# Order of the transposes, the value products and the weight sums in a fused attention and MLP kernel

## The chip, the cores and the metric

The kernel runs on one core of a Trainium2 chip. The core has five engines that run side by side, each taking its own instructions strictly in the order in which the program gives them: PE (TensorE, matmuls and transposes through the matrix array), DVE (VectorE), ACT (ScalarE), POOL (GpSimd) and SP (SyncE, which here only issues DMAs). An instruction waits until what it needs is ready, and everything behind it on its engine waits with it. The metric is device time in microseconds of the whole kernel; lower is better. The time before is 350.78 us, the median of three runs (350.43 to 350.84).

## The reference

```python
# 8 batches, 8 heads, 576 positions, head size 64
scores = scale * np.matmul(q, k.transpose(0, 1, 3, 2))
log_f = np.log(np.clip(f, 0.0001, 1.0))
cum = np.cumsum(log_f, axis=-1)
decay = cum[:, :, :, None] - cum[:, :, None, :]
scores = np.where(causal, -1000000000.0, scores + decay)
attn = np.exp(scores - np.max(scores, axis=-1, keepdims=True))
attn = attn / (np.sum(attn, axis=-1, keepdims=True) + 1e-09)
attn_out = np.matmul(attn, v)
# heads side by side: x is 4608 tokens x 512
h = x @ w_in          # 512 x 2048
g = h - np.tanh(h)
return g @ w_out      # 2048 x 512
```

## The kernel before

Attention goes by pairs of heads: 8 batches of 4 pairs, 32 in all, and each pair has a *slot* p (0 to 31; slot 32 finishes the last pair). The MLP runs in pieces between the attention's instructions, so that PE always has something to do.

**What a slot does.** For its pair it computes the scores in seven tiles, called s0 to s6 here (`scores`, L332 on PE): one or two matmuls into a PSUM bank, then an exp on ACT (L348). From slot 5 on, POOL sets the exp's upper triangle to zero (L359); in slots 0 to 4 a second matmul does the masking (L340). For the pair of the slot before, `values` multiplies the exps with v: two halves, va and vb, 15 matmuls each (L369), into one PSUM tile `av` of which there is a single buffer. Behind vb stand three DVE instructions (L375 to L377), here called the values chain: sums, their reciprocal, and `xn`, the normalised output. `turn` brings xn to the other orientation into `XR`: in batch 0 by five PE transposes and a DVE copy (L387, L388), later by two DMA transposes on SP's queue (L390, L392).

**Turns of q and k.** The scores need q and k with the head size on partitions. For batches 0 to 2, `trans` does this for the *next* pair: six PE transposes (L284) into a PSUM bank, then two copies, one for each head, into `QT` or `KT`, on DVE (L294, "VV") or ACT (L292, "AA" for slots 7 and 8; the very first two turns are split into four copies). From slot 4 on there is one such bank, `tr`, so a turn waits until the one before it is copied out; x's transposes in slot 4 use it as well. From batch 3 on, DMAs do the turning.

**The MLP.** Its work is a list of steps, 30 for each block of 512 tokens: 16 hidden tiles (`mlp1`: four matmuls L404, tanh on ACT L411, an addition `gt` on DVE L417, behind every fourth tile two more DVE sums L431) and 14 products (`product`, L452, eight matmuls each). The hidden tiles' PSUM banks `mb` are three in rotation; the tanh output has two buffers. The second matrix product is a fast algorithm in seven products for 2x2 blocks, n = 1 to 7, two row groups each. It needs four differences of blocks of w_out, which `wsum` makes once, on DVE (L266), in halves: sum 0 and, from it, sum 2 (for product 6), sum 1 (for product 7) and sum 3 (for product 4). They are put behind steps 16, 17, 19 and 21, both halves of a sum at once. `settle` (L469 to L483) takes the products out of PSUM; the results go through the tile `ost`, which has two buffers, to a DMA on SP's queue.

**The order.** Everything is emitted in an order written out by hand, and each engine takes its own in that order. Slots 0 to 4 follow the lists `FIRST`, whose entries `first_slot` decodes: s and g are score tiles and groups of them, q and k turns (the digit says how many slots ahead the pair is), va and vb the values, x the `turn` of the slot before and y that of two slots before, h0 to h2 the first three matmuls of the first three hidden tiles, m a step of the MLP, p memsets, r and c constant rows, and a number so many matmuls that only keep PE busy ("spins", L271). From slot 5 on, `att_items` lists a slot's entries: score tiles, loads, turns (in slots 5 to 10), va, vb and turn behind the second tile; and 6 steps (7 in slots 9 and 10, then 7 or 8) are spread evenly among those entries that count: the score tiles, the turns, vb and turn. By this rule, in slot 5 steps stand behind s1, turn, q's turn, s4, k's turn and s6. The products of the first block of tokens are steps 16 to 29: step 16 is the last of slot 6, 17 to 22 are slot 7's, 23 to 28 slot 8's, and step 29 is the first of slot 9.

Of the kernel before, what the change touches and what calls it, by code (L numbers as in the profile page):

```python
# [17 lines left out]
FAR = 3  # L18
# [4 lines left out]
def kernel(  # L23
# [18 lines left out]
    NPAIR = H // 2  # L42
# [4 lines left out]
    NFT = DFF // P  # L47
# [24 lines left out]
    K2, E2, T2 = NFT // 2, DM // 2, UW // 2  # L72
# [6 lines left out]
    qn, kn = ([t[0:S // NT6, :].rearrange("p (h n d) -> p h n d", h=H, n=NT6) for t in raw] for raw in (qraw, kraw))  # L79
    qb, kb = ([t[:, 0:NJ * DM].rearrange("p (n e) -> p n e", n=NJ) for t in raw] for raw in (qraw, kraw))  # L80
    vn = [qkp.tile([P, NJ, H, VW], FP16, tag=f"vn{i}", name=f"vn{i}") for i in range(2)]
    QT = [qkp.tile([D + 3, H, S], FP16, tag=f"QT{i}", name=f"QT{i}") for i in range(2)]
    KT = [qkp.tile([D + 3, H, PITCH], FP16, tag=f"KT{i}", name=f"KT{i}") for i in range(2)]
# [195 lines left out]
    def trans(b, c, src, dst, engs):  # L279
        pn, g3 = S // NT6, NT6 // 2  # L280
        t16 = t_bank().bitcast(FP16)[:, 0:2 * S // 2].rearrange("p (a g n) -> p a g n", a=2, g=g3)
        for a in range(2):
            for g in range(g3):
                nc.tensor.transpose(out=t16[:, a, g, :], in_=src[b % 2][:, 2 * c + a, 2 * g:2 * g + 2, :],  # L284
                                    identity=id16[0:pn, 0:pn])
        for a0, an in ((0, 1), (1, 1)) if len(engs) > 2 else ((0, 2),):
            for e in range(2):
                h0 = 2 * c + a0
                to = dst[b % 2][0:D, h0:h0 + an, 0:S].rearrange("d a (g e p) -> d a g e p", g=g3, e=2)[:, :, :, e, :]
                of = t16[e * D:(e + 1) * D, a0:a0 + an, :, :]  # L290
                if engs[2 * a0 + e] == "A":
                    nc.scalar.activation(out=to, in_=of, func=AF.Copy)  # L292
                else:
                    nc.vector.tensor_copy(out=to, in_=of)  # L294
            if a0 == 0 and engs == "AAAA":
                cum_q()
# [65 lines left out]
    def values(b, c, a):  # L362
        if a == 0:
            av = ps_av.tile([P, 2, 512], FP32, tag="av", name="av")
            AV[(b, c)] = av[:, :, 0:NJ * (D + 1)].rearrange("p a (i d) -> p a i d", i=NJ)
        av = AV[(b, c)]
        for ib in range(NJ):
            for j in range(ib + 1):
                nc.tensor.matmul(out=av[:, a, ib, :], lhsT=E.pop((b, c, a, j, ib)),  # L369
                                 rhs=vn[b % 2][:, j, 2 * c + a, 0:D + 1], start=(j == 0), stop=(j == ib))  # L370
        if a == 0:
            return
        xn = XN[(b, c)] = fin.tile([P, NJ, P], FP16, tag="xn", name="xn")
        rs = fin.tile([P, 2, NJ, 1], FP32, tag="rs", name="rs")
        nc.vector.tensor_scalar_add(out=rs, in0=av[:, :, :, D:D + 1], scalar1=1e-9)  # L375
        nc.vector.reciprocal(out=rs, in_=rs)
        nc.vector.tensor_tensor(out=xn.rearrange("p i (a d) -> p a i d", a=2), in0=av[:, :, :, 0:D],  # L377
                                in1=rs.to_broadcast([P, 2, NJ, D]), op=ALU.mult)

    def turn(b, c):  # L380
        xn = XN.pop((b, c))
        r0 = b % 3 * S
        if b == 0:
            xt = t_bank().bitcast(FP16)[:, 0:S]
            for ib in (NJ - 1, 0, 1, 2, 3):
                w0 = min(ib * P, S - P)
                nc.tensor.transpose(out=xt[:, w0:w0 + P], in_=xn[:, ib, :], identity=id16)  # L387
            nc.vector.tensor_copy(out=XR[:, c, r0:r0 + S], in_=xt)  # L388
            return
        nc.sync.dma_start_transpose(out=XR[:, c, r0:r0 + S - D].rearrange("p (n t) -> p n t", t=P),  # L390
                                    in_=xn[:, 0:NJ - 1, :].rearrange("p n d -> p (n d)"))
        nc.sync.dma_start_transpose(out=XR[:, c, r0 + S - D:r0 + S], in_=xn[D:P, NJ - 1, :])  # L392
# [96 lines left out]
    mlp = []  # L489
    for u in range(NU):  # L490
        mlp += [[(mlp1, u, ft)] for ft in turns]
        mlp += [[(product, u, n, g)] for n, g in ((1, 0), (1, 1), (2, 0), (6, 0), (6, 1), (2, 1))]
        mlp += [[(product, u, n, g)] for n in (5, 7, 3, 4) for g in range(2)]
    for at, n in ((NFT, 0), (NFT + 1, 2), (NFT + 3, 1), (NFT + 5, 3)):
        mlp[at] += [(wsum, n, 0, K2 // 2), (wsum, n, K2 // 2, K2)]

    STEPS = [0]

    def step():
        for fn, *args in mlp[STEPS[0]]:  # L500
            fn(*args)
        STEPS[0] += 1

    FIRST = [["8", "q0", "k0", "5", "s0", "s1", "q1", "s2", "k1", "p", "s4", "s5", "q2", "s6", "s3"],
# [4 lines left out]

    def first_slot(p):  # L510
        here = pairs[p]
        before = pairs[p - 1] if p else None
        for what in FIRST[p]:
            kind, arg = what[0], what[1:]
# [29 lines left out]
    def att_items(p):  # L544
        items = []
        before = pairs[p - 1]
        after = pairs[p + 1] if p + 1 < len(pairs) else None
        for ti in range(len(TILES)):
            if p < len(pairs):
                items.append((lambda ti=ti: scores(*pairs[p], (ti,), "late"), True))  # L550
            items += [(load, False) for load in LOADS.get((p, ti), ())]
            if ti in (3 if p == 2 * NPAIR - 1 else 2, 5) and after and after[0] < FAR:
                dst, src = (KT, kn) if ti == 5 else (QT, qn)
                items.append((lambda dst=dst, src=src: trans(*after, src, dst, "AA" if 2 * NPAIR - 1 <= p <= 2 * NPAIR else "VV"), True))
            if ti == 1:
                items += [(lambda a=a: values(*before, a), a == 1) for a in range(2)]
                items.append((lambda: turn(*before), True))
        return items

    with tc.manual_schedule(engines={PE, mybir.EngineType.Pool, mybir.EngineType.SP, mybir.EngineType.DVE,  # L560
                                     mybir.EngineType.Activation}):
        with tc.tile_pool(name="ps_t2", bufs=1, space=PSUM) as POOLS["t"]:
            with tc.tile_pool(name="ps_one", bufs=4, space=PSUM) as POOLS["s"]:
                first_slot(0)
            with tc.tile_pool(name="ps_two", bufs=2, space=PSUM) as POOLS["s"]:
                for p in range(1, NPAIR):
                    first_slot(p)
        del POOLS["t"]
        POOLS["s"] = ctx.enter_context(tc.tile_pool(name="ps_sc", bufs=2, space=PSUM))
        POOLS["m"] = ctx.enter_context(tc.tile_pool(name="ps_m", bufs=3, space=PSUM))  # L570
        first_slot(NPAIR)
        for p in range(NPAIR + 1, len(pairs) + 1):
            items = att_items(p)
            take = 6 if p <= 2 * NPAIR else 7 if p == 2 * NPAIR + 1 or p % 2 == 0 else 8
            whole, given, n = sum(c for _, c in items), 0, 0
            for emit, counts in items:
                emit()
                n += counts
                while given < take and (given + 1) * whole <= n * take and STEPS[0] < len(mlp):
                    step()  # L580
                    given += 1
        while STEPS[0] < len(mlp):
            step()
# [28 lines left out]
```

## Time and profile before

| what | us |
|---|---|
| median of three runs | 350.78 |
| the profiled execution, its own time | 350.38 |
| its span, from the first to the last instruction | 348.7 |
| PE busy | 334.7 (96%) |
| DVE busy | 253.3 (73%) |
| ACT busy | 220.2 (63%) |
| POOL busy | 176.9 (51%) |

The profile page shows one execution. A line of the timeline has the start, the duration, the engine, the line of the kernel, the operation, what is written and read, and the count where instructions in a row are merged; a bracket at its end says how long the engine was idle before it and what released it. Matmuls are pipelined and their ends are modelled, so that neighbouring ones overlap in the records: idle time is best read from the starts. The second part of the page cuts the span into 40 slices of 8.7 us and gives the busy share in tenths:

```profile
PE   7898998998999999999999999999999999999996
DVE  7576889819896589748984889388937863873872
ACT  6564876777765786568756875588558843623631
PEclk9989999999999999999999999999999999999999
```

PE's thinner slices are among the first ten, besides the last; DVE's row has one slice of 1, the ninth.

### The profile page before, as it was taken

The page shows a single profiled execution, that of the slowest core. Times are in us where ns is not written, and L with a number is a line of the kernel's source. Part 1 is how long each engine was busy: PE and PEld are TensorE (multiplying, and loading weights), DVE is VectorE, ACT ScalarE, POOL GpSimd, SP SyncE. Part 2 cuts the span into 40 slices and gives each one's busy share as a digit, 9 for nine tenths or more (in the row PEclk, how much of TensorE's full clock was granted, in tenths as well). Part 3 has the DMA queues.
Part 4 walks back from the last instruction along what each step waited for, and adds up shares of the span by engine and source line. Part 5 has one row for each costly group of instructions (what it writes and reads, how often), then busy time and mean ns, then how long its engine had stood idle before and what let it go on. Part 6 is the DMA issues. An engine that isn't in the chain of part 4 may idle for free.

```text
span 348.7 us, 8658 instructions
## 1 busy us (share of the span) xinstructions
PE 334.7 (96%) x3295; PEld 234.1 (67%) x3295; DVE 253.3 (73%) x523; ACT 220.2 (63%) x412; POOL 176.9 (51%) x322
## 2 busy tenths in 40 slices
PE   7898998998999999999999999999999999999996
PEld 2585556774578656887886568756887786487475
DVE  7576889819896589748984889388937863873872
ACT  6564876777765786568756875588558843623631
POOL 8967179875277726774667457753222220500500
PEclk9989999999999999999999999999999999999999
DMA  9999999999589998999699979994122013003003
GB/s 100 145 181 176 195 180 136 131 168 208 83 65 119 179 149 80 116 168 175 65 120 141 180 87 110 156 168 74 47 83 46 19 34 122 0 12 111 3 0 122
DMA packets 169560, 38.82 MB, mean 111 GB/s; under 512 B 155906, under 2 KB 169454, under 8 KB 169518
## 3 DMA queue, kind: packets, MB, share of 16 engines
q0 software_dynamic: 116576, 18.36, 87.2%
q1 hardware_dynamic: 52942, 19.90, 29.1%
q8 instruction: 26, 0.43, 0.6%
q14 instruction: 16, 0.13, 0.1%
HBM read 36.85 MB, written 9.44 MB: 133 GB/s over the span
## 4 chain that ended last, share of the span: by engine, by line
PE 78%; DVE 12%; DMA 4%; ACT 3%; issue 2%; SPq 1%; POOL 0%; DVEq 0%; ACTq 0%; POOLq 0%
PE mb L404 29%; PE px L452 16%; PE mb L452 12%; PE ps L332 11%; PE av L369 7%; DVE gt L417 4%; DMA out_dram<-ost 2%; DVE KT L294 2%; DVE sm L431 2%; DVE xn L377 1%; DMA kn<-in_k_dram 1%; ACT th L411 1%; ACT e L348 1%; PE t L284 1%; DVE QT L294 1%
## 5 line engine op out<-in xcount | busy, mean ns | idle before, releaser
L404 PE MATMUL mb<-XR,win 128*128 128x512 f16 (+4 forms) x704 | 141.6, 340 | 1.0 <-DVE gt L417 0.7
L348 ACT ACTIVATE e<-ps 128x512 f16<-128x512 f32 (+1 forms) x183 | 109.3, 617 | 28.2 <-PE ps L332 15.7
L411 ACT ACTIVATE th<-mb 128x512 f32<-128x512 f32 x144 | 86.3, 600 | 50.8 <-PE mb L404 46.5
L417 DVE TENSOR_TENSOR gt<-mb,th 128x512 f16<-128x512 f32 x144 | 97.1, 686 | 25.2 <-ACT th L411 24.4
L359 POOL TENSOR_SCALAR_AFFINE_SELECT e<-e 128x128 f16<-128x128 f16 x162 | 59.7, 372 | 104.5 <-ACT e L348 103.9
L404 PEld LDWEIGHTS <-win 128*128 128x128 f16 x704 | 61.8, 97 | 49.2 <-issue 2.8
L332 PE MATMUL ps<-QT,KT 67*128 67x64 f16 (+4 forms) x384 | 75.4, 279 | 4.3 <-DVE KT L294 1.4
L452 PEld LDWEIGHTS <-gt 128*128 128x128 f16 x576 | 53.8, 97 | 10.9 <-DVE gt L417 1.1
L332 PEld LDWEIGHTS <-KT 67*128 67x128 f16 x384 | 36.3, 99 | 26.4 <-DVE KT L294 3.4
L452 PEld LDWEIGHTS <-sm 128*128 128x128 f16 x432 | 40.4, 97 | 7.2 <-DVE ws L266 0.6
L452 PE MATMUL mb<-ws,gt 128*128 128x256 f16 x288 | 36.4, 272 | 0.0
L482 DVE TENSOR_TENSOR ost<-mb,part 128x512 f32<-128x512 f32 x25 | 17.1, 685 | 25.9 <-PE mb L404 6.8
L369 PEld LDWEIGHTS <-e 128*128 128x128 f16 x896 | 32.9, 98 | 3.7 <-DVE xn L377 0.9
L369 PE MATMUL av<-vn,e 128*128 128x65 f16 x896 | 34.4, 194 | 0.7 <-DVE xn L377 0.7
L469 ACT ACTIVATE part<-px 128x512 f32<-128x512 f32 x24 | 14.3, 597 | 30.1 <-PE px L452 30.1
L452 PE MATMUL px<-ws,sm 128*128 128x256 f16 x256 | 31.6, 272 | 0.0
L113 POOL DMA_DIRECT2D vn<-in_v_dram x32 | 28.7, 905 | 2.4 <-issue 1.9
L377 DVE TENSOR_TENSOR xn<-av,rs 128x640 f16<-128x640 f32 x32 | 26.4, 824 | 1.1
L431 POOL TENSOR_TENSOR sm<-gt 128x512 f16<-128x512 f16 x4 | 4.6, 1152 | 36.3 <-DVE gt L417 36.3
L94 POOL DMA_DIRECT2D qn<-in_q_dram x25 | 21.8, 872 | 1.5 <-issue 1.4
L94 POOL DMA_DIRECT2D kn<-in_k_dram x25 | 21.4, 854 | 1.2 <-issue 0.9
L452 PE MATMUL mb<-wout,gt 128*128 128x256 f16 x160 | 21.4, 272 | 0.0
(83 smaller groups left out, 302.6 us busy)
## 6 DMA issues: line engine op xcount, KB each, us to landing
out_dram<-ost SPq DMA_DIRECT2D x34, 256.0 KB
vn<-in_v_dram POOLq DMA_DIRECT2D x32, 128.0 KB, 5.9
qn<-in_q_dram POOLq DMA_DIRECT2D x20, 128.0 KB, 3.8
kn<-in_k_dram POOLq DMA_DIRECT2D x20, 128.0 KB, 4.7
win<-in_moe_w_in_dram POOLq DMA_DIRECT2D x4, 512.0 KB, 8.6
wout<-in_moe_w_out_dram POOLq DMA_DIRECT2D x2, 1024.0 KB, 16.3
qn<-in_q_dram POOLq DMA_DIRECT2D x10, 144.0 KB, 7.4
kn<-in_k_dram POOLq DMA_DIRECT2D x10, 144.0 KB, 7.1
```

The costliest lines, as they stand in the source:

```text
L94: nc.gpsimd.dma_start(out=dst[b % 2][0:pn, n, :].rearrange("p (h d) -> p h d", h=H), in_=src[b, :, n * P:n * P + pn, :].rearrange("h p d - ...
L113: nc.gpsimd.dma_start(out=vn[b % 2][:, n, h0:h1, 0:D], in_=v[b, h0:h1, n * P:(n + 1) * P, :].rearrange("h p d -> p h d"))
L332: nc.tensor.matmul(out=ps[:, col:col + n], lhsT=KT[b % 2][0:D + 3, h, j * P:(j + 1) * P], rhs=QT[b % 2][0:D + 3, h, i0:i0 + n], start=True ...
L348: nc.scalar.activation(out=eb[:, :, lo:hi], in_=banks[:, 0:n2, lo:hi], func=AF.Exp, scale=qscale)
L359: nc.gpsimd.affine_select(out=view, in_=view, compare_op=ALU.is_ge, fill=0.0, base=0, pattern=pat, channel_multiplier=-1)
L369: nc.tensor.matmul(out=av[:, a, ib, :], lhsT=E.pop((b, c, a, j, ib)), rhs=vn[b % 2][:, j, 2 * c + a, 0:D + 1], start=(j == 0), stop=(j == ib))
L377: nc.vector.tensor_tensor(out=xn.rearrange("p i (a d) -> p a i d", a=2), in0=av[:, :, :, 0:D], in1=rs.to_broadcast([P, 2, NJ, D]), op=ALU. ...
L404: nc.tensor.matmul(out=hps[:, o:o + n], lhsT=win[:, ci, ft * P:(ft + 1) * P], rhs=XR[:, ci, t:t + n], start=(ci == 0), stop=(ci == NCH - 1))
L411: nc.scalar.activation(out=th, in_=hps, func=AF.Tanh, scale=-1.0)
L417: nc.vector.tensor_tensor(out=GT[(u, ft)], in0=hps, in1=th, op=ALU.add)
L452: nc.tensor.matmul(out=ps[:, g * E2:(g + 1) * E2], lhsT=left(k), rhs=right[:, k, :], start=(first and (g == 0 or last) and k == 0), stop=( ...
L482: nc.vector.tensor_tensor(out=ost, in0=ps, in1=PART.pop((u, {2: 1, 7: 5, 4: 6}[n])), op=ALU.add)
```

## The change

Five places change, all in the order of emission; every computation stays.

- At the start, 3 spins behind k's first turn instead of 5.
- In slots 2 and 3, vb is emitted ahead of k's turn instead of behind it.
- In slot 4, x comes ahead of h2 and q's turn (it stood behind both), and k's turn ahead of the third step instead of behind it.
- In slots 5 to 10, q's turn comes behind the second score tile, ahead of the values (it stood behind the third tile; in slot 7 behind the fourth), and k's behind the fifth tile (it stood behind the sixth). The steps between them fall in other places by the rule of even spreading: in slots 5 to 8 behind s1, vb, s2, s4, s5 and s6; in slots 9 and 10 behind s1, vb, turn, s3, s4, s5 and s6.
- The halves of each weight sum go to two successive steps: sum 0 to steps 14 and 15 (both were behind 16), sum 2 to 16 and 17 (17), sum 1 to 19 and 20 (19), sum 3 to 22 and 23 (21).

```diff
-    for at, n in ((NFT, 0), (NFT + 1, 2), (NFT + 3, 1), (NFT + 5, 3)):
-        mlp[at] += [(wsum, n, 0, K2 // 2), (wsum, n, K2 // 2, K2)]
+    for at, n in ((NFT - 2, 0), (NFT, 2), (NFT + 3, 1), (NFT + 6, 3)):
+        for o in range(2):
+            mlp[at + o] += [(wsum, n, o * K2 // 2, (o + 1) * K2 // 2)]
...
-    FIRST = [["8", "q0", "k0", "5", "s0", "s1", "q1", "s2", "k1", "p", "s4", "s5", "q2", "s6", "s3"],
+    FIRST = [["8", "q0", "k0", "3", "s0", "s1", "q1", "s2", "k1", "p", "s4", "s5", "q2", "s6", "s3"],
              ["g0", "g1", "k1", "g3", "va", "r", "vb", "q2", "g2"],
-             ["g0", "y", "va", "g1", "k1", "vb", "g3", "q2", "g2"],
-             ["g0", "y", "va", "g1", "k1", "vb", "g3", "g2"],
-             ["c", "va", "s0", "y", "vb", "s1", "h0", "h1", "q1", "h2", "x", "s2", "m", "s3", "m", "s4", "m", "k1", "s5", "m", "s6", "m"]]
+             ["g0", "y", "va", "g1", "vb", "k1", "g3", "q2", "g2"],
+             ["g0", "y", "va", "g1", "vb", "k1", "g3", "g2"],
+             ["c", "va", "s0", "y", "vb", "s1", "h0", "h1", "x", "h2", "q1", "s2", "m", "s3", "m", "s4", "k1", "m", "s5", "m", "s6", "m"]]
...
-            if ti in (3 if p == 2 * NPAIR - 1 else 2, 5) and after and after[0] < FAR:
-                dst, src = (KT, kn) if ti == 5 else (QT, qn)
+            if ti in (1, 4) and after and after[0] < FAR:
+                dst, src = (KT, kn) if ti == 4 else (QT, qn)
                 items.append((lambda dst=dst, src=src: trans(*after, src, dst, "AA" if 2 * NPAIR - 1 <= p <= 2 * NPAIR else "VV"), True))
```

## The prediction

> **What bounds the kernel now.** The page first (its lines on engines and slices, above), then the busy time of the engines by stretch: PE, PEld, DVE, ACT, POOL, then the granted clock, DMA share and GB/s. Then the timelines of PE, DVE and ACT up to 95 us.
>
> ```profile
> 0.00:31.00 31.00, 26.16 (x311) 17.78 (x312) 20.68 (x58) 19.07 (x29) 25.72 (x36) 0.94 1.86 146
> 31.00:95.00 64.00, 59.11 (x590) 37.79 (x589) 49.77 (x102) 45.62 (x88) 39.58 (x71) 1.00 2.02 161
> 95.00:348.00 253.00, 249.41 (x2397) 178.56 (x2396) 182.84 (x365) 155.52 (x296) 111.61 (x216) 1.00 0.87 95
> ```
>
> PE idles 4.8 us before 31 us and 4.9 us in 31 to 95, where all the edits lie; behind 95 us it is busy 98.6% of the time with code that doesn't change. So whatever slot 11 starts earlier or later by is the change of the total. At most about 9 us are to be had.
>
> ```profile
> 37.50:47.65 10.15, 9.49 (x87) 5.10 (x85) 9.81 (x20) 8.43 (x17) 5.50 (x11) 1.00 1.39 201
> 47.65:56.30 8.65, 8.14 (x82) 5.04 (x83) 7.54 (x16) 6.10 (x13) 6.63 (x13) 1.00 2.68 153
> 56.30:68.10 11.80, 10.55 (x127) 8.36 (x126) 11.59 (x23) 8.51 (x17) 10.56 (x17) 1.00 3.07 131
> 68.10:78.60 10.50, 9.90 (x133) 8.04 (x129) 1.90 (x4) 6.94 (x13) 7.98 (x15) 1.00 2.34 157
> ```
>
> The third busy column is DVE. In slots 5 to 7 (37.5 to 68.1 us) it is busy 28.9 of 30.6 us: reordering its queue there gains only what ends its few idle spells. In slot 8 it is nearly idle, and that is a wait, not rest (below).
>
> **The change part by part.** I follow one shift from slot to slot: minus is earlier than before. A turn's two DVE copies take 0.91 us, one values chain on DVE (rs, its reciprocal and xn: from 23.9 to 25.2 below) 1.2 us, half a weight sum 0.68 us.
>
> *Two spins fewer.*
>
> ```profile
> 7.22 2.33 PE L271 MATMUL spin<-ones 128*128 128x512 f16 x5
> 7.46 1.28 DVE L294 COPY KT<-t 64x288 f16<-64x288 f16 x4
> 9.34 0.63 PE L332 MATMUL ps<-QT,KT 67*128 67x512 f16 x1
> 6.88:10.29 3.41, 3.41 (x14) 1.48 (x14) 1.71 (x5) 1.45 (x4) 3.41 (x6) 1.00 2.27 148
> ```
>
> Spins start 0.42 us apart (9.34 less 7.22 over 5), so three end at 8.49; k's copies are done at 8.74, and s0 starts at 8.79 instead of 9.34. But these matmuls run at half rate until 10.29 (the same 67x512 matmul shows 0.63 us here and 0.38 in the row at 24.37 below), so s0's three wide ones just fill the time: s1 starts at 10.2, not 10.52, partly slow. Shift -0.28. PE is unbroken from there to the next copies, so it lasts into slot 2.
>
> *Values ahead of k's turn, slots 2 and 3.*
>
> ```profile
> 22.94 0.92 DVE L294 COPY KT<-t 64x576 f16<-64x576 f16 x2 [0.87 <-PE t L284]
> 24.35 0.82 DVE L377 TENSOR_TENSOR xn<-av,rs 128x640 f16<-128x640 f32 x1
> 24.37 0.38 PE L332 MATMUL ps<-QT,KT 67*128 67x512 f16 x1
> 29.34 0.59 PE L369 MATMUL av<-vn,e 128*128 128x65 f16 x14 [0.70 <-DVE xn L377]
> 29.80 0.38 PE L332 MATMUL ps<-QT,KT 67*128 67x512 f16 x1
> ```
>
> DVE takes k's copies, then the values chain; now the other way round. With vb ended at 22.85 the chain runs from 22.9 to 24.1 and the copies end at 25.0. Slot 3's first scores need them: 25.06 instead of 24.37, +0.69. In slot 3 everything follows; its chain ends at 28.87 instead of 29.29, so slot 4's va no longer waits 0.70 us, but k's copies end at 29.7 and s0 of slot 4 starts at 29.8 as before. What the spin gave is used up: shift 0.
>
> *x ahead of h2 and q1, k1 ahead of a step, slot 4.*
>
> ```profile
> 31.46 0.82 DVE L377 TENSOR_TENSOR xn<-av,rs 128x640 f16<-128x640 f32 x1
> 32.38 0.42 PE L284 MATMUL t<-id,qn 96*128 96x96 f16 x6
> 33.82 0.45 PE L387 MATMUL t<-id,xn 128*128 128x128 f16 x5 [0.37 <-DVE QT L294]
> 34.65 0.60 ACT L348 ACTIVATE e<-ps 128x512 f16<-128x512 f32 x1 [2.77 <-PE ps L340]
> 37.50 0.69 DVE L417 TENSOR_TENSOR gt<-mb,th 128x512 f16<-128x512 f32 x1 [0.29 <-ACT th L411]
> ```
>
> q1 and x share one PSUM bank, and x now waits for q's copies. With x at 32.38 (its xn is ready at 32.28), its copy ends at 33.33, under h2; q1 follows at 33.38 and s2 at 33.64 instead of 34.11. ACT, which is packed from 34.65 on, starts 0.47 earlier. Then k's copies go ahead of the third gt and fill the 0.29 us that DVE waited there. Together -0.47 - 0.29 = -0.76, and DVE stays packed to slot 5's end: K ready for slot 6 at -0.73.
>
> *q behind the second tile, k behind the fifth; weight sums in parts.*
>
> ```profile
> 47.68 0.61 PE L332 MATMUL ps<-QT,KT 67*128 67x512 f16 x3 [0.45 <-DVE KT L294]
> 54.10 0.41 PE L284 MATMUL t<-id,kn 96*128 96x96 f16 x6 [0.48 <-DVE QT L294]
> 57.96 1.38 DVE L266 TENSOR_TENSOR ws<-wout 128x1024 f16<-128x1024 f16 x2
> 59.60 1.37 DVE L266 TENSOR_TENSOR ws<-wout,ws 128x1024 f16<-128x1024 f16 x2
> 59.91 0.60 ACT L348 ACTIVATE e<-ps 128x512 f16<-128x512 f32 x1 [1.46 <-PE ps L332]
> 60.34 1.29 PE L452 MATMUL mb<-ws,sm 128*128 128x256 f16 x8 [0.47 <-DVE ws L266]
> 64.69 1.30 ACT L292 ACTIVATE KT<-t 64x576 f16<-64x576 f16 x2
> 66.05 0.39 PE L332 MATMUL ps<-QT,KT 67*128 67x512 f16 x1 [0.39 <-ACT KT L292]
> 68.88 0.17 DVE L375 TENSOR_SCALAR rs<-av 128x10 f32<-128x10 f32 x1 [0.85 <-PE av L369]
> ```
>
> The waits of k's trans for q's copies (0.48 us in slot 6, shorter in 7, 9 and 10) go. But k's copies keep their place among DVE's instructions (behind four gts, ahead of two), so with DVE packed the next slot's start gains nothing: PE waits for K instead. In slot 6 the first half sum (step 14) even enters ahead of them: +0.68 less rounding, slot 7 starts at -0.13. The work isn't lost. DVE reaches the second half of sum 2 at 60.2 instead of 60.99 (-0.8), and PE, with q already turned, meets no wait at 60.34. In slot 7 both turns are copied on ACT: q now in an idle spell (ACT waited 1.46 us ahead of 59.91), k at 62.5 to 63.8 instead of 64.69 to 66.0, so slot 8's s0 starts about 64.4 (its bank waits for the sixth exp) instead of 66.05, its vb ends about 67.3, q's 0.26 us included. DVE, packed, is free at 67.25. The values chain of slot 8 starts at 67.33 instead of 68.88: **-1.55**.
>
> *What hangs on it.*
>
> ```profile
> 72.79 5.76 DMA out_dram<-ost
> 81.24 0.60 ACT L411 ACTIVATE th<-mb 128x512 f32<-128x512 f32 x1 [0.76 <-DVE gt L417]
> 85.70 0.61 PE L332 MATMUL ps<-QT,KT 67*128 67x512 f16 x3 [0.71 <-DVE KT L294]
> ```
>
> Slot 8's xn feeds two transposes on SP's queue, behind them the output DMA; it lands 5.76 us later, and only then has DVE a free ost buffer. This is why DVE idles in slot 8, and slot 9 is packed from there to its K copies: slot 10 starts 7.15 us behind the landing (85.70 less 78.55). So -1.55 passes on if the landing takes as long as now. In slot 9 q's copies now stand ahead of the chain and the first gt: gt comes 0.91 later, the tile that needs its bank also, and this tile's matmuls and tanh outlast the two gts left: four matmuls at half a spin's 0.42 are 0.85, the last one's drain 0.17 (0.38 less 0.21), tanh 0.6, 1.65 with a handover, against two gts of 0.6: DVE idles 0.45. Slot 10 starts at -1.1, slot 11 as well, since slot 10 has two sums and two gts in that place (2.05 us). On SP's and POOL's queues nothing changes its order: the transposes that x becomes in later slots and the loads stand behind the same tiles. The nearest landing is v's for slot 1:
>
> ```profile
> L105 POOL DMA_DIRECT2D vn<-in_v_dram x1: 729/729/729, 11.2 to 11.2; - x1
> ...
> DMA to landing us min/median/max: 5.5/5.5/5.5
> ```
>
> it is there at 16.7, and its values start at 17.0 by the shift.
>
> **Sum:** -0.28 + 0.28 - 0.76 + 0.6 (slot 6) - 1.4 (slots 7, 8) + 0.45 = -1.1 us. The profiled execution took 350.38 us (span 348.7 and 1.7 around it); the four known ones average 350.6, so 349.5. Bounds for the terms: slots 2 and 3 between -0.86 (all of va's wait gone) and +0.69; slots 7 and 8 between 0 and -2.1.
>
> **Rivals.**
>
> ```profile
> 13.70:17.12 3.42, 2.31 (x26) 1.51 (x24) 2.35 (x10) 2.21 (x5) 3.42 (x6) 1.00 2.53 148
> 17.12:20.53 3.41, 3.39 (x47) 3.03 (x47) 2.60 (x9) 1.05 (x2) 3.41 (x5) 0.50 1.92 172
> 27.36:30.77 3.41, 2.44 (x51) 1.89 (x48) 2.02 (x6) 2.09 (x4) 3.09 (x4) 1.00 2.16 170
> ```
>
> 1. *The half-clock spell goes.* A thin window is followed by one at 0.50. With PE 0.28 earlier, dense values matmuls move into the thin window, and the next may stay at full clock: 3.39 us of matmuls in 1.7, less 0.2 taken above: -1.1 - 1.5, 348.0. For: PE was the chain there. Against: nothing says how much it takes; the stretch from 27.36 is hardly denser, and the clock behind it stays full (1.00 from 31 to 95). The Trainium skill (TensorE: Matmul & The Clock Gate, Part 1) has the clock fall after an idle window; here it fell after one that was 68% busy by the modelled ends, so the trace disagrees.
>
> 2. *The output lands no sooner: slower.* Place: the output DMA of slot 8, issued near 71.2 instead of 72.79.
>
> ```profile
> DMA to landing us min/median/max: 7.8/8.7/10.1
> ...
> DMA to landing us min/median/max: 5.2/5.9/6.4
> ```
>
> The first row is q's blocks issued from 58.8 to 64.6, the second k's from 67.7 to 73.6: the backlog is drained between. If it doesn't move with the kernel, the output takes some 8.3 (between the first row's least and its median) instead of 5.76 us, and ost starts at +0.95; with slot 9's 0.45, +1.4: 352.0. It decides from a landing of 6.9 us on, where the gain is zero. Against: the loads are issued behind the same tiles and move too. The Trainium skill (DMA: Bandwidth & Descriptors, Issuing engines are not separate DMA queues) has all issuers share 16 engines and interleave, which would let this happen.
>
> 3. *Waits only change places.* DVE's packed slots keep their ends, and PE's and ACT's earlier work in slot 7 ends at the same sums: 350.6. For: slots 5, 6 and 10 by the reckoning above.
>
> 4. *Full clock one window later.* Before, PE had no hole in 6.88 to 10.29; now one of 0.3 us. The next window's work at half rate costs 1.6 us: +0.5, 351.1. The Trainium skill's Part 1 wants some 3.4 us of sustained work, by which this is what three spins would bring.
>
> **How the numbers follow.** Forecast 0.42, rival 1 0.18, rival 2 0.21, rival 3 0.13, rival 4 0.06. Range: rival 1 with another 1 us of slots 2 to 4 below (347.0), and rival 2 with a little (352.3) above; the forecast's own is 348.7 to 350.3. A measurement tells 0.2% (0.7 us) from no change, so faster needs a gain over 0.7: 0.33 from the forecast, 0.18 from rival 1, 0.03 from rival 3, 0.54 together. Slower: 0.18 from rival 2, 0.04 from rival 3, 0.03 from rival 4 and 0.01 from the forecast, 0.26. Within 0.2%: 0.20, what is left of each.
>
> **What would show it.** Right: slot 3's first scores wait for K; x at the end of h1, with the first exp of s2 near 34.2; in slot 7 a wait for K but none for ws; DVE's wait in slot 8 ending near 77; slot 11 from about 93.9. Wrong: a clock of 1.00 in 17 to 20.5 (rival 1), an output landing of 7 us or more (rival 2), the start of slot 8 still near 66 (rival 3), 512-wide matmuls of 0.43 us behind 10.3 (rival 4).

## The result, and the profile after

| | before | after |
|---|---|---|
| median, us (12 executions each) | 350.77 (349.66 to 351.18) | 353.36 (351.41 to 354.75) |
| the profiled execution, us | 350.38 | 351.41 |
| its span, us | 348.7 | 349.7 |

The change makes the kernel slower by 2.6 us: ratio 1.0079, 95% interval 1.0061 to 1.0097. The forecast of 349.5 was wrong, and 353.36 lies above its range too. The profiled execution is the fastest of the twelve; what the others add comes below.

The page of the changed kernel, busy tenths of 40 slices and the granted clock:

```profile
PE   6788999976999999999999999999999999999996
DVE  7676989809897489848884889378937873873872
PEclk9999999999999999999999999999999999999999
DMA  9999999999979998999699999993122014003003
```

DVE's empty slice is still the ninth (now 0), and PE has a thin one of its own there and in the tenth (7 and 6; before 9 and 8). The DMA engines are busy for 90% or more of every slice up to the eleventh. The busy time by stretch of the changed kernel (PE, PEld, DVE, ACT, POOL, clock, DMA share, GB/s), first the stretches shown of before, then slot 8 from its values chain to the next output sum:

```profile
0.00:31.00 31.00, 24.14 (x319) 16.34 (x320) 21.78 (x61) 19.73 (x30) 24.97 (x35) 1.00 1.86 145
31.00:95.00 64.00, 56.89 (x577) 36.84 (x576) 48.33 (x95) 44.12 (x86) 40.21 (x71) 1.00 2.03 162
95.00:348.00 253.00, 250.36 (x2402) 178.94 (x2400) 183.86 (x368) 156.56 (x298) 111.74 (x217) 1.00 0.85 94
66.30:78.80 12.50, 10.22 (x113) 7.76 (x112) 1.94 (x6) 7.46 (x14) 7.57 (x15) 1.00 2.32 145
```

Between 31 and 95 us PE now idles 7.1 us instead of 4.9. In the last row DVE works 1.94 us of 12.50: before it was 1.90 of 10.50. The hole of slot 8 begins some 2 us sooner and does not end sooner. The timeline of PE, changed kernel: first scores (L332) of slots 0, 3, 6, 7, 8, 10 and 11, x in slot 4 (L387), and of slot 9's hidden tiles (L404) the end of the first together with the second, then the third and the fourth:

```profile
8.15 0.39 PE L332 MATMUL ps<-QT,KT 67*128 67x512 f16 x1 [0.28 <-DVE KT L294]
23.25 0.39 PE L332 MATMUL ps<-QT,KT 67*128 67x512 f16 x1 [0.77 <-DVE KT L294]
30.91 0.44 PE L387 MATMUL t<-id,xn 128*128 128x128 f16 x5
45.40 0.61 PE L332 MATMUL ps<-QT,KT 67*128 67x512 f16 x3 [0.34 <-DVE KT L294]
54.79 0.61 PE L332 MATMUL ps<-QT,KT 67*128 67x512 f16 x3 [0.73 <-DVE KT L294]
63.25 0.87 PE L332 MATMUL ps<-QT,KT 67*128 67x512 f16 x3
76.60 1.24 PE L404 MATMUL mb<-XR,win 128*128 128x512 f16 x5 [1.01 <-DMA XR<-xn]
79.53 1.02 PE L404 MATMUL mb<-XR,win 128*128 128x512 f16 x4 [1.42 <-DVE ost L482]
82.27 1.02 PE L404 MATMUL mb<-XR,win 128*128 128x512 f16 x4 [1.49 <-DVE gt L417]
86.58 0.61 PE L332 MATMUL ps<-QT,KT 67*128 67x512 f16 x3 [0.86 <-DVE KT L294]
96.17 0.61 PE L332 MATMUL ps<-QT,KT 67*128 67x512 f16 x3
```

The timeline of DVE, changed kernel, slot 8's values chain and the start of slot 9:

```profile
66.34 0.15 DVE L375 TENSOR_SCALAR rs<-av 128x10 f32<-128x10 f32 x1
...
78.79 0.69 DVE L482 TENSOR_TENSOR ost<-mb,part 128x512 f32<-128x512 f32 x1 [9.87 <-DMA out_dram<-ost]
79.40 0.91 DVE L294 COPY QT<-t 64x576 f16<-64x576 f16 x2
...
81.54 2.09 DVE L417 TENSOR_TENSOR gt<-mb,th 128x512 f16<-128x512 f32 x3
83.96 0.69 DVE L417 TENSOR_TENSOR gt<-mb,th 128x512 f16<-128x512 f32 x1 [0.33 <-ACT th L411]
```

And the chain of waits of the changed kernel between the two:

```profile
66.78 0.84 DVE xn L377
67.63 1.25 SPq L390
68.92 1.22 SPq L392
70.24 8.43 DMA out_dram<-ost
78.79 0.69 DVE ost L482
```

The values chain runs 2.54 us sooner than before (66.34 against 68.88) and the output DMA is issued 2.55 us sooner (70.24 against 72.79), but it takes 8.43 us to land instead of 5.76. So the last output sum, step 29, starts at 78.79; before it started at 78.67. The kernel before, that sum on DVE and slot 11's first scores on PE:

```profile
78.67 0.69 DVE L482 TENSOR_TENSOR ost<-mb,part 128x512 f32<-128x512 f32 x1 [6.83 <-PE mb L404]
```

```profile
94.96 0.63 PE L332 MATMUL ps<-QT,KT 67*128 67x512 f16 x3
```

The bracket of the first line names PE, but the product for this sum had ended at 76.83 (75.79 and 1.04 long); what ended last was the landing, at 78.55. All that slots 0 to 8 won is gone at this one wait. Behind it slot 10 begins 7.79 us later (86.58 less 78.79; before 7.03) and slot 11 another 9.59 (before 9.26): +1.1 us together, and with the 0.12 of the landing 1.21 at slot 11's start, against 1.0 on the whole span.

### The profile page after: what moved, and what is told of

It reads as the page before. It is cut to its first block, busy times and chain, and to the rows that moved or that the text cites. A ratio compares the mean times of both kernels' runs of the same rounds, so it can differ in the third digit from the quotient of the medians.

```text
span 349.7 us, 8651 instructions
## 1 busy us (share of the span) xinstructions
PE 331.4 (95%) x3293; PEld 232.1 (66%) x3293; DVE 254.0 (73%) x523; ACT 220.4 (63%) x412; POOL 176.9 (51%) x322
## 4 chain that ended last, share of the span: by engine, by line
PE 78%; DVE 11%; DMA 5%; ACT 3%; issue 1%; SPq 1%; DVEq 0%; ACTq 0%
PE mb L404 30%; PE px L452 16%; PE mb L452 13%; PE ps L332 11%; PE av L369 7%; DMA out_dram<-ost 3%; DVE gt L417 3%; DVE sm L431 2%; DVE KT L294 2%; DVE xn L377 1%; ACT e L348 1%; ACT th L411 1%; DMA KT<-cc 1%; DMA ws<-in_f_dram 1%; DVE ws L266 1%
## 5 line engine op out<-in xcount | busy, mean ns | idle before, releaser
L404 PE MATMUL mb<-XR,win 128*128 128x512 f16 (+4 forms) x704 | 141.4, 340 | 4.9 <-DVE gt L417 2.3
L404 PEld LDWEIGHTS <-win 128*128 128x128 f16 x704 | 62.0, 97 | 54.8 <-issue 7.7
L332 PE MATMUL ps<-QT,KT 67*128 67x64 f16 (+4 forms) x384 | 74.6, 277 | 6.9 <-DVE KT L294 3.0
L332 PEld LDWEIGHTS <-KT 67*128 67x128 f16 x384 | 35.8, 98 | 27.3 <-DVE KT L294 5.9
L369 PE MATMUL av<-vn,e 128*128 128x65 f16 x896 | 33.6, 193 | 0.0
L369 PEld LDWEIGHTS <-e 128*128 128x128 f16 x896 | 31.9, 97 | 2.4
L375 DVE TENSOR_SCALAR rs<-av 128x10 f32<-128x10 f32 x32 | 5.2, 162 | 22.5 <-PE av L369 22.3
```

What stands on the lines that cost most here:

```text
L332: nc.tensor.matmul(out=ps[:, col:col + n], lhsT=KT[b % 2][0:D + 3, h, j * P:(j + 1) * P], rhs=QT[b % 2][0:D + 3, h, i0:i0 + n], start=True ...
L404: nc.tensor.matmul(out=hps[:, o:o + n], lhsT=win[:, ci, ft * P:(ft + 1) * P], rhs=XR[:, ci, t:t + n], start=(ci == 0), stop=(ci == NCH - 1))
```

## The experiments

Two theories. L: the landing of slot 8's output is fixed by the backlog of loads on the shared DMA engines, DVE waits for it, PE runs dry in slot 9, and a half-clock spell may follow. S: the three spins cost clock at the start. "Ost" below is the start of step 29's output sum on DVE, "issue" that of the output DMA ahead of it. Each ratio is against the kernel before, timed beside it (medians 350.58 to 350.88).

| run | median, us (lowest to highest, executions) | ratio, 95% interval | issue | ost |
|---|---|---|---|---|
| e1_again | 352.88 (351.83 to 353.57, 6) | 1.0065, 1.0050 to 1.0080 | 71.22 | 78.66 |
| e2_spin5 | 353.57 (351.95 to 355.10, 6) | 1.0083, 1.0058 to 1.0109 | 72.11 | 78.87 |
| e3_turns | 351.48 (350.40 to 352.00, 12) | 1.0023, 1.0012 to 1.0033 | 71.98 | 79.10 |
| e4_ost3 | 347.29 (346.88 to 348.42, 5) | 0.9912, 0.9898 to 0.9925 | 70.33 | 73.92 |
| e5_before_ost3 | 349.09 (347.72 to 350.38, 12) | 0.9954, 0.9932 to 0.9976 | 72.32 | 76.01 |
| e6_kb_later | 348.58 (1) | none | 70.72 | 74.91 |
| e7_out_on_act | 353.74 (1) | none | 69.18 | 78.43 |
| e8_ost3_mixed | 347.81 (346.94 to 348.77, 6) | 0.9924, 0.9898 to 0.9949 | 70.27 | 73.95 |
| e9_before_turns | 352.97 (352.06 to 353.49, 7) | 1.0052, 1.0031 to 1.0073 | 70.89 | 78.09 |
| e10_kb_later_timed | 349.36 (348.68 to 351.13, 12) | 0.9953, 0.9936 to 0.9971 | 71.83 | 76.41 |
| e11_before_kb_later | 349.31 (348.05 to 350.98, 12) | 0.9962, 0.9943 to 0.9980 | 71.57 | 75.41 |
| e12_ost3_kb_later | 347.74 (347.26 to 347.91, 6) | 0.9904, 0.9880 to 0.9929 | 71.05 | 74.53 |
| e13_filler | 351.47 (350.61 to 353.32, 12) | 1.0035, 1.0014 to 1.0056 | 71.12 | 78.78 |

**The changed kernel again, and with five spins.** The first has no edit; the second takes the spins back.

> The changed kernel once more, to see a second trace of it and the granted clock beside the time of every execution. Theory L (landing): slot 8's output DMA is issued sooner but lands near 78.6 us as before, PE runs ahead and then stands still for over 4 us in slot 9, and in most executions a half-clock spell follows; the trace has DVE's ost of step 29 at 78 to 80 us, and if this execution is a slow one (over 353 us) it has 0.50 somewhere behind 78 us. Theory S (start): with three spins the array gets its full clock late or loses it at the start; a slow execution has its 0.50 ahead of 25 us and slot 9 like the first trace. Ratio 1.006 to 1.010 by both.

```diff
-    FIRST = [["8", "q0", "k0", "3", "s0", "s1", ...
+    FIRST = [["8", "q0", "k0", "5", "s0", "s1", ...
```

> The changed kernel with the five spins of before. Theory L: the start is 0.3 to 1.2 us later, the landing stays, so the hole in slot 9 is shorter by that and the total hardly moves: ratio 1.004 to 1.010. Theory S: the slow executions go, ratio at most 1.003, and the spread of the times falls from 3 us to about 1.5 us.

With five spins the time is no better (1.0083), so S falls. The second trace of the changed kernel shows something that the first has not. Its page, the clock, and its stretches of 3.41 us around the tenth slice:

```profile
PEclk9999999998999999999999999999999999999999
```

```profile
78.68:82.09 3.41, 1.24 (x5) 0.48 (x5) 3.30 (x8) 0.86 (x3) 2.29 (x4) 1.00 1.63 197
82.09:85.50 3.41, 3.37 (x14) 1.52 (x14) 2.08 (x4) 2.18 (x4) 1.10 (x3) 0.50 1.70 212
```

Here a window in which PE was busy for 1.24 of 3.41 us lies at the output wait, and the next one runs at 0.50. The first trace of the changed kernel has windows with more work in them at that place, and none at half clock:

```profile
76.93:80.35 3.42, 2.00 (x13) 0.98 (x11) 1.52 (x4) 1.85 (x4) 0.97 (x2) 1.00 1.47 222
80.35:83.76 3.41, 1.92 (x15) 0.97 (x14) 3.08 (x6) 1.45 (x3) 1.74 (x4) 1.00 1.79 139
```

From slot 10 on the second trace runs 0.58 us behind the first (87.16 against 86.58):

```profile
87.16 0.61 PE L332 MATMUL ps<-QT,KT 67*128 67x512 f16 x3
```

The start's clock does not matter here: the trace of e2_spin5 has half clock from 15.06 to 18.47, and its slot 10 begins at 86.65, only 0.07 behind the first trace of the changed kernel, which has no such spell. The wait for the landing swallows the difference.

**The turns.** Their old places in the changed kernel, and their new places alone in the kernel before.

```diff
-            if ti in (1, 4) and after and after[0] < FAR:
-                dst, src = (KT, kn) if ti == 4 else (QT, qn)
+            if ti in (3 if p == 2 * NPAIR - 1 else 2, 5) and after and after[0] < FAR:
+                dst, src = (KT, kn) if ti == 5 else (QT, qn)
```

> The changed kernel with the turns of q and k in slots 5 to 10 where they were before (behind the third or fourth and the sixth tile). Theory L: q's copies no longer stand ahead of the first gt in slot 9 and PE runs ahead less, so slot 10 starts at most 7.2 us behind the landing instead of 7.9: ratio 0.997 to 1.003. Theory S: the loss stays, 1.005 to 1.010.

> The kernel before with the new places of q's and k's turns alone. Theory L: the landing stays near 78.7 us, and slot 10 starts 7.8 us behind it instead of 7.0, with the hole in slot 9 and its half-clock spell in some executions: ratio 1.003 to 1.009, most of the loss. Rival (the loss is spread over the edits, or comes from the weight sums): at most 1.002.

With the turns back the kernel loses 0.0023, with the turns alone 0.0052: they carry most of the 0.0079, the other edits a little. With them back, slot 10 begins 7.02 us behind ost, as before (7.03), though ost itself is no sooner (79.10). The stretches of the kernel with the turns alone:

```profile
77.40:80.82 3.42, 1.30 (x8) 0.48 (x5) 2.61 (x6) 1.07 (x3) 2.08 (x4) 1.00 1.67 210
80.82:84.23 3.41, 2.66 (x13) 1.31 (x13) 2.12 (x5) 1.69 (x3) 1.33 (x3) 0.50 1.60 216
84.23:87.64 3.41, 3.41 (x12) 1.32 (x11) 2.93 (x6) 1.69 (x3) 0.70 (x2) 0.50 1.82 172
```

Again a window with 1.30 us of work, then two at half clock; slot 10 begins at 87.81, 1.23 us behind the first trace of the changed kernel, though ost came 0.70 sooner (78.09).

**Take the wait away: a third buffer for ost.** In both kernels, in a pool of its own.

```diff
+    osp = ctx.enter_context(tc.tile_pool(name="osp", bufs=3))
...
-        ost = tmp.tile([P, DM], FP32, tag="ost", name="ost") if half != 1 else PART.pop((u, n, "ost"))
+        ost = osp.tile([P, DM], FP32, tag="ost", name="ost") if half != 1 else PART.pop((u, n, "ost"))
```

> The changed kernel with three buffers for ost instead of two, so that step 29's addition waits for no landing. Theory L: DVE's wait of 9.9 us goes, slot 10 starts before 84 us, and with it the hole in slot 9: ratio 0.990 to 0.997, spread small. Theory S: only the wait's own 1 us goes, the slow executions stay: 1.003 to 1.008.

> The kernel before with three ost buffers, nothing else. Theory L: without the wait for the landing slot 9 starts its DVE work when step 29 is multiplied, near 77 us instead of 78.7, so the gain is 1 to 2 us, ratio 0.994 to 0.997; the five edits are then worth what lies between this and the changed kernel with three buffers (0.991), 1 to 2 us, as the prediction had it without the landing. Against L: if the third buffer had its gain elsewhere, this one gains as much as that one, 0.991 or less.

The timelines of DVE and of PE, changed kernel with three buffers (lines are one higher):

```profile
73.92 0.69 DVE L483 TENSOR_TENSOR ost<-mb,part 128x512 f32<-128x512 f32 x1 [4.89 <-PE mb L453]
```

```profile
82.36 0.61 PE L333 MATMUL ps<-QT,KT 67*128 67x512 f16 x3 [0.74 <-DVE KT L295]
```

The releaser of the output sum is PE's product now, no DMA, and slot 10 begins at 82.36 instead of 86.58. The same buffer takes 0.0046 off the kernel before and 0.0167 off the changed one (1.0079 less 0.9912). What separates the two without the wait is 0.0042 or 1.5 us, near the 1.1 that the prediction's sum gave the edits, but not all of it is the order. The mean granted clock of every execution is on record: all five of e4_ost3 have 0.999 or more; of the twelve of e5_before_ost3 five have (median 347.95 us), and seven have 0.989 to 0.995 (median 350.07). Its trace, one of the seven, is at half clock from 15.27 to 18.68. At full clock the two kernels are 0.7 us apart (347.29 and 347.95, five executions each). Whether the edits help to keep the clock is not shown: with three buffers and edits undone (e8_ost3_mixed, below) three of six executions have less than 0.998, with both cures (e12_ost3_kb_later) one of six.

**What fixes the landing.** k's blocks of the third batch are loaded six tiles later; and, in another kernel, ACT's queue issues that output DMA, past the transposes on SP's.

```diff
-            at_tile(p0, n, lambda b=b, n=n: load_block(kb, k, b, n))
+            at_tile(p0, n + (6 if b == FAR else 0), lambda b=b, n=n: load_block(kb, k, b, n))
```

> The changed kernel with k's five block loads for batch 3 six tiles later (out of slot 8 into slot 9), so that fewer bytes stand ahead of slot 8's output. If the shared DMA engines' backlog sets the landing: step 29's addition starts before 77.5 us (78.7 to 79.1 in six traces so far), the output lands at most 6.5 us behind its issue. If the landing is bound to something that these loads do not touch (the transposes on the same queue, above all): it stays at 78.5 to 79.2.

```diff
-        nc.sync.dma_start(out=out[r0:r0 + T2, e0:e0 + E2].rearrange("(g p) e -> p g e", p=P),
-                          in_=ost.rearrange("p (g e) -> p g e", g=2))
+        eng = nc.scalar if u == 0 and n == 7 else nc.sync
+        eng.dma_start(out=out[r0:r0 + T2, e0:e0 + E2].rearrange("(g p) e -> p g e", p=P),
+                      in_=ost.rearrange("p (g e) -> p g e", g=2))
```

> The changed kernel with slot 8's output DMA issued by ACT instead of SP, so that it does not stand behind SP's transposes on their queue. If SP's queue holds it: it lands within 5 us of its issue, step 29's addition starts before 76 us. If the shared engines' backlog does: the start stays within 1 us of 78.7.

Time from issue to landing of the block loads issued from 64 to 74 us, first in the kernel before (k's five and one of q's), then in the changed kernel (k's five); in the third fence k's five in the kernel with the later loads; then DVE's timeline of that kernel, and the chain of waits of the one with the output on ACT:

```profile
L94 POOL DMA_DIRECT2D kn<-in_k_dram x5: 689/891/897, 67.7 to 73.6; - x5
L94 POOL DMA_DIRECT2D qn<-in_q_dram x1: 692/692/692, 64.6 to 64.6; - x1
...
DMA to landing us min/median/max: 5.2/6.1/7.8
```

```profile
L94 POOL DMA_DIRECT2D kn<-in_k_dram x5: 689/891/898, 65.5 to 70.7; - x5
...
DMA to landing us min/median/max: 7.6/10.2/10.8
```

```profile
L94 POOL DMA_DIRECT2D kn<-in_k_dram x5: 715/881/892, 73.7 to 81.9; - x5
```

```profile
74.91 0.69 DVE L482 TENSOR_TENSOR ost<-mb,part 128x512 f32<-128x512 f32 x1 [5.61 <-DMA out_dram<-ost]
```

```profile
69.18 9.13 DMA out_dram<-ost
```

Issued 2.04 us sooner than in e1_again and from another engine, the output still lands at 78.31: neither SP's queue nor the time of issue decides (one execution). With the five loads out of the way (73.7 to 81.9 instead of 65.5 to 70.7) the output, issued at 70.72, is there by 74.91, after 4.2 us at most; in a second execution, e10_kb_later_timed, it is issued at 71.83 and there by 76.41, after 4.6 at most. And in the first trace of the changed kernel the loads beside it slow as well, from a median of 6.1 us to 10.2 (8.2 in its second trace, where two of q's are among the seven). What it shares with them are the 16 DMA engines. This agrees with the Trainium skill (DMA: Bandwidth & Descriptors, Issuing engines are not separate DMA queues), which has the transfers of all issuers interleave on the same engines.

**The same two cures again, timed and combined.**

> The changed kernel with the five loads six tiles later, timed. Theory L: the landing at about 75 us makes the changed kernel faster than before, ratio 0.992 to 0.996, with a small spread. If the one look was a lucky execution: 0.998 or more.

> The kernel before with the same five loads six tiles later. Theory L: the output lands before step 29 is multiplied, so it gains about what three ost buffers gave it: ratio 0.994 to 0.998, and step 29's addition starts near 76 to 77 us. The edits are then worth 0.002 to 0.005 on this footing too.

> The changed kernel with both, three ost buffers and the later loads. Theory L: both take away the same wait, so together they bring little over one: ratio 0.988 to 0.993. If the backlog holds up something else as well (slot 8's XR transposes, for which PE waited 1.0 us in the first trace): below 0.988.

Later loads bring both kernels to the same time (0.9953 and 0.9962, intervals that overlap), which is 0.0126 off the changed kernel and 0.0038 off the kernel before. On this footing the edits bring next to nothing, a miss, since 0.002 to 0.005 was expected. The output sums of e11_before_kb_later and of e10_kb_later_timed:

```profile
75.41 0.69 DVE L482 TENSOR_TENSOR ost<-mb,part 128x512 f32<-128x512 f32 x1 [5.08 <-PE mb L452]
```

```profile
76.41 0.69 DVE L482 TENSOR_TENSOR ost<-mb,part 128x512 f32<-128x512 f32 x1 [6.19 <-DMA out_dram<-ost]
```

In the kernel before the wait for the landing is gone: PE's product releases the sum (at 75.41, where 76 to 77 was expected). In the changed kernel half a microsecond of it is left: its product ends at 75.89, and at 74.44 in e6_kb_later, and the sums start at 76.41 and 74.91. The two traces of this kernel also show what half clock at the start costs without the long wait: e10_kb_later_timed has it from 14.79 to 18.20, e6_kb_later has none, and slot 11 begins at 94.02 and 92.50, 1.5 us apart. How much of the miss the rest of the wait makes isn't settled. Both cures together give 0.9904, little more than the third buffer alone, as L has it, since they take away the same wait.

**Three buffers with some edits undone**: k ahead of vb again in slots 2 and 3, and q behind the third tile in slots 9 and 10.

```diff
-             ["g0", "y", "va", "g1", "vb", "k1", "g3", "q2", "g2"],
-             ["g0", "y", "va", "g1", "vb", "k1", "g3", "g2"],
+             ["g0", "y", "va", "g1", "k1", "vb", "g3", "q2", "g2"],
+             ["g0", "y", "va", "g1", "k1", "vb", "g3", "g2"],
...
-            if ti in (1, 4) and after and after[0] < FAR:
+            if ti in (2 if p > 2 * NPAIR else 1, 4) and after and after[0] < FAR:
```

> The changed kernel with three ost buffers, with k's turn ahead of vb again in slots 2 and 3, and q's turn behind the third tile, behind the values, in slots 9 and 10 only. If the reckoning by DVE's queue holds (values ahead of k cost 0.3 to 0.7 us, q ahead of the first gt costs 0.45 in slot 9): ratio 0.986 to 0.990, that is 0.4 to 1.5 us less than with three buffers alone (0.991). If PE or ACT set those slots, 0.991 again.

A miss: 0.9924 against 0.9912, with intervals that overlap, so what the two edits cost once DVE waits for no landing is too little for the medians. Two things are undone at once, and only the traces tell them apart: slot 10 begins 8.25 us behind ost instead of 8.44 in e4_ost3, so that q's early copies in slot 9 cost 0.19 there, not 0.45.

**Is it the half clock?** The changed kernel, with 16 more matmuls on PE ahead of three hidden tiles of slot 9; their banks are written over by the tiles.

```diff
+        if u == 1:
+            for _ in range({turns[0]: 4, turns[1]: 6, turns[2]: 6}.get(ft, 0)):
+                nc.tensor.matmul(out=hps, lhsT=ones16[:, 0:P], rhs=ones16[:, 0:UW])
```

> The changed kernel with 16 matmuls more in slot 9 (4, 6 and 6 ahead of its first three hidden tiles, into the same PSUM banks, which the tiles' own first matmul then clears), which only keep PE busy while it waits there. If the half-clock spells that follow the hole make the difference between the first trace (351.4) and the median (353.4): no trace has 0.50 behind 75 us, the slow executions go, median 351.0 to 352.2 and ratio 1.001 to 1.005. If the spells cost nothing, since everything there waits for DVE: median 353 or more, as the matmuls cannot save time otherwise.

Busy time by stretch and PE's timeline of this kernel:

```profile
75.00:82.00 7.00, 7.00 (x48) 3.35 (x45) 3.10 (x7) 1.85 (x4) 2.10 (x4) 1.00 1.99 161
```

```profile
86.57 0.61 PE L332 MATMUL ps<-QT,KT 67*128 67x512 f16 x3 [0.86 <-DVE KT L294]
```

PE is full, slot 10 begins where it did in the first trace of the changed kernel (86.58), the clock stays at 1.00, and the median falls to 1.0035, or 1.2 us above before: what the first trace shows without a spell (1.0). Against 1.0079 the intervals are apart, against 1.0065 they overlap a little. So the half clock adds about 1.1 to 1.5 us to the changed kernel's median. The granted clocks agree: seven of the twelve executions here have a mean of 1.00 (median 351.43 us) and five have 0.990 to 0.995 (median 352.98); of the changed kernel's twelve only one has 1.00, the profiled one. So the extra matmuls don't take away every spell.

## Why the prediction was wrong

- **The failed step** is "So -1.55 passes on if the landing takes as long as now." The landing took 8.43 us instead of 5.76. The wait ended at 78.79 where the prediction had it "near 77". The price of this step is all that stood ahead of it. Rival 2, "The output lands no sooner: slower", had the mechanism and its place. That its 8.3 us met the 8.43 is in part luck: it reckoned with an issue near 71.2, and in e1_again, issued at 71.22, the output took 7.31 and ost started where it had before, not at +0.95. What spoke against it, that the loads move too, was the error: they do move (65.5 to 70.7 instead of 67.7 to 73.6), but they too take longer to land (7.6 to 10.8 us instead of 5.2 to 6.4). The runs show that the landing keeps its time: in the kernel before and in six others that have the wait and the early loads, ost starts from 78.09 to 79.10 us, with issues from 69.18 to 72.79.
- **The start.** The first scores came at 8.15, sooner than the 8.79 foreseen: they need the first two of k's four copies alone. The first full clock was at 5.26 us in this execution, at 10.29 in that of before, and from 4.55 to 10.73 over the traces, whether with three spins (5.26, 10.41) or five (4.82, 10.29): it differs from execution to execution, and the 2 us that slot 2 began sooner are not the spins'. The clock from 17 to 20.5, 0.50 before, was 1.00 in this execution: that is the sign given for rival 1. Its gain was luck of the execution (with three spins e3_turns has such a spell, with five e11_before_kb_later has none), and it was lost at the landing as well.
- **Slots 2 and 3**: +0.59, foreseen +0.28; the wait for K was there in slot 3 (0.77 at 23.25, foreseen 0.69); slot 4's first scores, which the prediction had wait for K too, waited 0.55 for an exp instead. **Slot 4**: x 2.58 us behind the slot's first scores, as foreseen; from slot 4 to slot 6 -0.81, foreseen -0.76. **Slot 6** +0.76, foreseen +0.6. **From slot 7 to slot 8's chain** -1.02, foreseen -1.4. In slot 7 PE waited for K (0.73 at 54.79) and not for ws, as foreseen. From slot 4 to slot 8's chain that is -1.07, foreseen -1.56: the gain was real up to there.
- **Slot 9** was mis-sized: +0.76 instead of +0.45. The mechanism is the one given: q's copies first (79.40), three gts behind them, then DVE waits for a tanh (0.33). But PE had by then waited 1.42 us for ost and 1.49 for gt: with its early work done in slot 8, its hidden tiles are what DVE waits for. **Slot 10** had been set to nothing and cost 0.33: on DVE three gts in a row took 2.10 us and one sum 0.63 instead of 0.47; what slowed them the runs don't show.
- **Left out** altogether was that PE, waiting in slot 9, would lose its clock. The row for it stood in the prediction (a window with 2.31 of 3.42 us, then 0.50) but was used for the start alone. In the trace of the kernel before, PE had work left for slot 9 and kept full clock there.
- **The sum, mended**: +0.12 at the landing, +0.76, +0.33, and 0.2 back by the end: +1.0, the first trace. The median lies 2.0 above the first trace. The spells take 1.1 to 1.5 of that. Some of the rest comes at the very end, which the prediction took for code that passes slot 11's shift on unchanged: there the last additions wait for another output to land, 2.66 us in the first trace and 3.74 in the second:

```profile
346.08 0.83 DVE L476 TENSOR_TENSOR ost<-mb,part 128x256 f32<-128x256 f32 x2 [2.66 <-DMA out_dram<-ost]
```

```profile
347.73 0.76 DVE L476 TENSOR_TENSOR ost<-mb,part 128x256 f32<-128x256 f32 x2 [3.74 <-DMA out_dram<-ost]
```

No trace shows the five executions above 354 us, but their mean clocks are on record: 0.988 or 0.989, the same as in the two traces with two windows at half clock (e7_out_on_act, e9_before_turns). One of 351.66 us has 0.989 as well, one of e1_again took 353.57 at 1.00, and the kernel with the extra matmuls has some up to 353.3. So the clock is not all of it, and this part stays open.

## What to carry to other kernels

Where the path goes through a DMA's landing, ask what is queued beside it before passing a gain through: a transfer issued sooner into a backlog lands when the backlog is drained, and work drawn forward ahead of that wait leaves a hole behind it. Here one more buffer for the output (0.9912, with later loads 0.9904) was worth more than all the edits in the order, and turned their loss of 0.0079 into a gain of 0.0042 (1.5 us, of which 0.7 are left at full clock). An engine that wins time ahead of a fixed wait also loses its filling behind it, and PE can lose its clock there.

## What the runs showed of the hardware

- Three traces have a window of 3.41 us in which PE was busy for 1.24 to 1.30 us, and all three have half clock behind it, for one window (e1_again) or two (e9_before_turns, e7_out_on_act). Windows of 1.92 and 2.00 us passed without, and yet the kernel before lost its clock behind one of 2.31, and four other traces lost it at the start behind windows of 1.89 to 2.35 us (e2_spin5, e3_turns, e5_before_ost3, e10_kb_later_timed). So busy time by the modelled ends doesn't give the bound, and what does is open. The Trainium skill (TensorE: Matmul & The Clock Gate, Part 1) ties the fall to an idle window; none of these was. The same part of the Trainium skill has the window run free of the kernel, which agrees with the spread of the first full clock above.
- What a spell in slot 9 costs is read from ost on, since ost itself starts at different times. Slot 10's values begin 9.35 us behind it in the first trace of the changed kernel, 10.07 in e1_again, 11.28 in e9_before_turns and 11.30 in e7_out_on_act: 0.7 us for one window of 3.41 at half clock, 1.9 for two. A window full of work loses half its length, 1.7, but in the first trace PE waited 0.86 us for K ahead of slot 10 (86.58), and in e1_again it does not wait there: part of the loss fell into a wait that was there anyway.
